# Attention: the first pairs' row maxima, two heads in one tile and one reduction, under another set of planner constants

## The chip, the cores and the metric

The kernel runs on one core of a Trainium2 chip. The metric is device time in microseconds, the median of several executions. Five engines run side by side, each with its own instruction stream in a fixed order: TensorE (PE; its weight loads are PEld), VectorE (DVE), ScalarE (ACT), GpSimd (POOL) and SyncE (SP, which here issues the transfers). They wait for one another by semaphores.

## The reference

Inputs: q, k and v of 4 x 8 heads x 1152 x 64, and the weights of two further layers. Neighbouring rows of q are averaged, so each head has 576 queries and 1152 keys. Per head: scores = q k^T / 8, minus the row maximum, exp, divided by the row sum, times v. The result goes as 2304 tokens x 512 through a dense layer (`h * cos(h)` between two products) and then through 8 experts, of which each token takes the one with the largest gate. Only the attention is touched by the change.

```python
scores = scale * np.matmul(q_pool, k.transpose(0, 1, 3, 2))
scores = scores - np.max(scores, axis=-1, keepdims=True)
attn = np.exp(scores)
attn = attn / (np.sum(attn, axis=-1, keepdims=True) + 1e-09)
return np.matmul(attn, v).astype(np.float32)
```

## The kernel before

**Work.** The 32 heads are taken as 16 pairs; head 0 of a pair lies on partitions 0 to 63, head 1 on 64 to 127. Each pair has two passes over its scores.

The first pass finds the row maxima in rounded copies (`KH`, `QH`, made by ScalarE in `kh` and `qh`). Queries come in four tiles `t` of 128 and a rest of 64 per head (`t` = 4; both heads' rest share one tile through `QT`, made by `qt`), keys in three groups `g` of 384. A tile `(t, g)` is one product per head into a bank of its own of a pair of banks, and VectorE reduces it to the maxima `MX`. `mneg` takes the maximum over the three groups, negated, `pmr` transposes it on TensorE, `mrow` copies it, and `mset` writes it by four small transfers into a row `MR`. For pair 0 tiles 0 to 2 come first and go into `MR` by a quicker way (`pmq`, `mput`); its tiles 3 and 4 follow as a second part (`lo` = 3), whose row is needed for the second half of pair 0's queries alone.

The second pass takes the queries in two halves `hq` of 288 and the keys in nine blocks `j` of 128: `s` puts scores plus the row `MR` into PSUM, `exp` (ScalarE) makes `E`, `es` (GpSimd) adds the nine `E` up for the row sums, `pv` multiplies by v. Per half follow `ob`, `sum`, `ln`, `rcp`, `nr1`, `nr2` and `norm`. GpSimd has the `es` (8 a half), `qadd` (the averaging of q) and `norm`.

**Buffers.** PSUM: two bank pairs for `s`, one bank pair for the maxima (`ps_x`, tag "x"), one bank for `o`, one small. SBUF: 14 `E`, 4 K, 3 Q, 2 each of `KH`, `QH`, `QT`, raw q.

**The first pairs' maxima, as they are now.** In the second part of pair 0 and in all of pair 1 the tile is taken apart: `mx1` (lines 278 to 287) makes the product of one head into one half of a bank pair `T["xe"]` that these steps share, and `red1` (294 to 296) reduces that half, 128 x 384; the halves alternate (`nx % 2`). All other tiles go by `mx` (266 to 276) and `red` (298 to 305), both heads in one bank pair and one reduction of 128 x 768; only tile (4, 2) has one bank.

**Order.** `steps` (37 to 126) lists every step with a due time, an engine, a cost, what it reads and writes and its buffer. The due times count in units of which a pair has six: pair `i` starts at `b = 6*i`, `s` of half `hq` and block `j` is due at `b + 3*hq + j/3`. The rest is set by constants: `p` for the casts, another `p` for the maxima, `SPREAD` over which their 14 tiles are spread, `BEHIND` for `pv`. The conversions of the dense layer's weights (`cabs`, `c1` to `c4`, `chi`, `clo`, stores `cst`) are 32 jobs `n` with due times of their own. `plan` (129 to 184) is a greedy list scheduler: at each turn, per engine, it looks at the steps due at most `AHEAD` after the engine's first pending one, and takes the one with the least of wait x `WAIT` + due time (+ `SWITCH` on TensorE, where the kind of product changes); over all engines the earliest start goes next. It skips steps whose inputs haven't been placed. The order so found is written out as each engine's fixed order; what the planner thinks of durations has no other effect.

```python
late = max(0, t - free[e])*WAIT + P[n][0] + SWITCH*(e == "PE" and P[n][4] != mode)
seen[n] = end[n] + LAND[e] + FETCH.get(p[2], 0)
```

The dense layer and the experts (`moe`) follow the attention in the same program.

Of the kernel before, what the change touches and what calls it, by code (L numbers as in the profile page):

```python
# [8 lines left out]
F32 = mybir.dt.float32  # L9
# [16 lines left out]
COLS, ROWS = "PEc", "PEr"  # L26
LAND = {"PE": 0.27, "ACT": 0.07, "DVE": 0.07, "POOL": 0.07, "SP": 1.9}
FETCH = {"load": 3.0, "loadv": 2.0, "cload": 2.0}
AHEAD = {"PE": 4.5, "DVE": 3.78, "ACT": 3, "POOL": 3.61, "SP": 8.0}
CHANGE = {COLS: 0.2, ROWS: 0.1}  # L30
EARLY = 4
BEHIND = 1.54
SPREAD = 5.1
WAIT, SWITCH = 6.04, 0.85


def steps(NP, NJ, J):


    P, nx = [], 0  # L40

    def at(t, name, args, eng, cost, reads=(), writes=(), buf=None):
        P.append((t, len(P), name, args, eng, cost, list(reads), list(writes), buf))

    tiles = [(t, g) for t in range(4) for g in range(3)] + [(4, 0), (4, 2)]
    for i in range(NP):
        b = 6*i
        first = i == 0
        p = -101 if first else b - 10.75
        early = -200 if i < 2 else b - 20.8  # L50
        at(early, "load", (i, 0), "SP", 0.6, (), [("qr", i, 0)], ("qr", 2, ("qr", i, 0)))
        at(early, "load", (i, 1), "SP", 0.6, (), [("k", i, 0)], ("k", 4, ("k", i, 0)))
        if first:
            at(early, "load", (i, 2), "SP", 0.6, [("k", i, 0)], [("k", i, 1)])
            at(early, "load", (i, 3), "SP", 0.6, [("qr", i, 0)], [("qr", i, 1)])
        at(-200 if first else b - 7, "loadv", (i,), "SP", 0.6, (), [("v", i)], ("v", 3, ("v", i)))
        whole = range(1 + first)
        for x in whole:
            c = ((0.67, 0.33)[x] if first else 1)
            at(p + -0.49 + 9*x, "qadd", (i, x), "DVE" if first and not x else "POOL", 1.45*c, [("qr", i, x)] + [("q", i, 0)]*x, [("q", i, x)], None if x else ("q", 3, ("q", i, 0)))  # L60
            at(p + 0.1 + 9*x, "qh", (i, x), "ACT", 0.2 + 0.47*c, [("q", i, x)] + [("qh", i, 0)]*x, [("qh", i, x)], None if x else ("qh", 2, ("qh", i, 0)))
        for x in range(2):
            c = ((0.48, 0.76)[x] if first else 0.67)
            at(p + (0.1 if first else 0.2 + 0.8*x), "kh", (i, x), "ACT", c, [("k", i, x*first)] + [("kh", i, 0)]*x, [("kh", i, x)], None if x else ("kh", 2, ("kh", i, 0)))
        at(-4 if first else p + 0.98, "qt", (i,), "ACT", 0.48, [("q", i, whole[-1])], [("qt", i % 2)])
        parts = ((0, 3), (3, 5)) if first else ((0, 5),)
        for lo, hi in parts:
            p = (-4 if lo else -100) if first else b - 8.47
            for n, (t, g) in enumerate(tiles):
                if lo <= t < hi:  # L70
                    x = p + n*(0.1 if first else SPREAD/14)
                    ks = [[("kh", i, 0)], [("kh", i, 0), ("kh", i, 1)], [("kh", i, 1)]][g]
                    if t == 4: ks = [("kh", i, 0), ("kh", i, 1), ("qt", i % 2)]
                    else: ks = ks + [("qh", i, x) for x in whole if t == 3 or not x]
                    key = ("x", i, t, g)
                    if lo or i == 1:
                        for h in range(2) if t < 4 else (0, 1)[:3-g]:
                            half = ("x", nx % 2)
                            at(x, "mx1", (i, t, g, h, nx % 2), ROWS, 0.19, ks + [("xe",)]*(nx > 0), [half] + [("xe",)]*(nx == 0), None if nx else ("x", 1, ("xe",)))
                            at(x, "red1", (i, t, g, h, nx % 2), "DVE", 0.56, [half, ("xe",)], [("mx", i, lo)])  # L80
                            nx += 1
                        continue
                    at(x, "mx", (i, t, g), ROWS, 0.35 if (t, g) == (4, 0) else 0.19, ks, [key], ("s", 2, key) if p == -100 and n % 3 else ("x", 1, key))
                    at(x + 0.08, "red", (i, t, g), "DVE", 0.56 if (t, g) == (4, 2) else 0.96, [key], [("mx", i, lo)])
            x = (-2 if lo else p + 2) if first else p + SPREAD
            at(x, "mneg", (i, lo, hi), "DVE", 0.17, [("mx", i, lo)], [("mneg", i, lo)])
            if first and not lo:
                at(x + 0.1, "pmq", (i,), ROWS, 1.2, [("mneg", i, lo)], [("pmr", i, lo)], ("m", 1, ("pmr", i, lo)))
                for h in range(2):
                    at(x + 0.2, "mput", (i, h), ("DVE", "ACT")[h], 0.45, [("pmr", i, lo)], [("mr", i, h - 2)])  # L90
                continue
            at(x + 0.1, "pmr", (i, lo, hi), ROWS, 0.2, [("mneg", i, lo)], [("pmr", i, lo)], ("m", 1, ("pmr", i, lo)))
            at(x + 0.2, "mrow", (i, lo, hi), "DVE", 0.27, [("pmr", i, lo)], [("mrow", i, lo)])
            at(x + 0.2, "mset", (i, lo, hi), "SP", 2.4, [("mrow", i, lo)], [("mr", i, lo)])
        for hq in range(2):
            for j in range(J):
                m = b + 3*hq + j/3
                mr = [("mr", i, x) for x in ([-2, -1] + [3]*hq if first else [0])]
                key = (i, hq, j)
                at(m, "s", key, ROWS, 0.617, [("k", i, x) for x in whole] + [("q", i, x) for x in whole if x < 1 or hq] + mr, [("s", *key)], ("s", 2, ("s", *key)))  # L100
                at(m + 0.17, "exp", key, "ACT", 0.65, [("s", *key)], [("e", *key)], ("e", 14, ("e", *key)))
                if j:
                    at(m + 0, "es", key, *(("DVE", 0.8) if (i, hq) == (NP-1, 1) and j > 4 else ("POOL", 1.45)), [("e", *key)] + [("e", i, hq, 0)]*(j == 1), [("es", i, hq)], ("es", 2, ("es", i, hq)) if j == 1 else None)
                at(m + BEHIND, "pv", key, COLS, 0.486, [("v", i), ("e", *key)], [("o", i, hq)], ("o", 1, ("o", i, hq)) if j == 0 else None)
            m = b + 3*hq + max(3.9, BEHIND + 2.7)
            key = (i, hq)
            at(m + -0.11, "ob", key, "ACT", 0.41, [("o", *key)], [("ob", *key)], ("ob", 2, ("ob", *key)))
            at(m + 0.1, "sum", key, COLS, 0.486, [("es", *key)], [("sum", *key)], ("m", 1, ("sum", *key)))
            at(m + 0.5, "ln", key, "ACT", 0.5, [("sum", *key)], [("ln", *key)], ("ln", 2, ("ln", *key)))
            at(m + 0.46, "rcp", key, "ACT", 0.44, [("ln", *key)], [("r0", *key)], ("r0", 2, ("r0", *key)))  # L110
            at(m + 0.3, "nr1", key, "DVE", 0.46, [("sum", *key), ("r0", *key)], [("nr", *key)], ("nr", 2, ("nr", *key)))
            at(m + 0.6, "nr2", key, "DVE", 0.46, [("r0", *key)], [("nr", *key)])
            at(m + 0.54, "norm", key, "POOL", 0.95, [("nr", *key), ("ob", *key)], [("xT", *key)])
    for n in range(NJ):
        x = 10.76 + 3.01*n if n < 27 else 89 + 1.2*(n - 27)
        at(x - 5, "cload", (n,), "SP", 0.6, (), [("ct", n)], ("ct", 2, ("ct", n)))
        at(x, "cabs", (n,), "ACT", 0.65, [("ct", n)], [("ca", n)], ("m", 1, ("ca", n)))
        for c in range(1, 5):
            at(x + 0, f"c{c}", (n,), "DVE", 0.69, [("ct", n)], [("ca", n)])
        at(x + 0.27, "chi", (n,), "ACT", 0.58, [("ca", n)], [("co", n)], ("co", 2, ("co", n)))  # L120
        at(x + 0, "clo", (n,), "DVE", 0.69, [("ca", n)], [("co", n)])
        at(x + 0.1, "cst", (n,), "SP", 1.2, [("co", n)], [("ws", n)])
        f = n - 4*(n//8) - 4
# [63 lines left out]
def attention(nc, tc, q, k, v, xT, ident, w_in, w_out, ws, x2d, W1):  # L187
# [7 lines left out]
    KG = 384  # L195
# [3 lines left out]
    with ExitStack() as ctx:  # L199
# [75 lines left out]
                for x, gg in enumerate(range(g, min(g+2, 3))):  # L275
                    nc.tensor.matmul(p[:, x, :KG], lhsT=QT[i % 2], rhs=KH[:, gg*KG:(gg+1)*KG], start=True, stop=True)

        def mx1(i, t, g, h, b):

            if "xe" not in T:  # L280
                T["xe"] = ps_x.tile([128, 2, 512], F32, tag="x", name="pmx")
            p = T["xe"][:, b, :KG]
            KH, QH = T["kh", i], T["qh", i]
            if t < NT4:
                nc.tensor.matmul(p, lhsT=QH[R[h], t*128:(t+1)*128], rhs=KH[R[h], g*KG:(g+1)*KG], start=True, stop=True)
            else:
                nc.tensor.matmul(p, lhsT=QT[i % 2], rhs=KH[:, (g+h)*KG:(g+h+1)*KG], start=True, stop=True)

        def maxima(i):
            if ("mx", i) not in T:  # L290
                T["mx", i] = sm.tile([128, 27], F32, tag="MX", name="MX")
            return T["mx", i]

        def red1(i, t, g, h, b):
            o = 24+g+h if t == NT4 else 3*(2*t+h)+g
            nc.vector.reduce_max(maxima(i)[:, o:o+1], T["xe"][:, b, :KG], axis=AX.X)

        def red(i, t, g):
            p = T.pop(("x", i, t, g))
            out = maxima(i)  # L300
            if t < NT4:
                nc.vector.reduce_max(out.rearrange("p (w g) -> p w g", g=3)[:, 2*t:2*t+2, g], p[:, :, :KG], axis=AX.X)  # L302
            else:
# [721 lines left out]
```

## Time and profile before

| | us |
|---|---|
| median of 3 runs | 1232.14 |
| lowest, highest | 1231.37, 1232.37 |
| profiled execution, its own time | 1230.01 |
| its span, first to last instruction | 1228.3 |
| attention within it | to about 482 |

The span is the part of the profiled execution that the trace covers; 1.7 us lie around it. Rows of the timeline give the start (us from the start of the span), the duration, engine, line, operation, output <- input, the number of instructions merged into the row, and in brackets the engine's idle time before it and who ended it. A row of several instructions lasts from the first start to the last end. Rows of groups give the busy time and the mean of one in ns. TensorE's products overlap, and their ends are modelled.

### The profile page before, as it was taken

Reading aid. Unit: us, or ns where it says so; the run is one execution under the profiler, and the core shown is the slowest. Engines: PE = TensorE matmul, PEld = TensorE weight load, DVE = VectorE, ACT = ScalarE, POOL = GpSimd, SP = SyncE. Lnnn points to the kernel's source line nnn. Section 1 sums busy time; section 2 is a strip of 40 time slices with the busy share of each in tenths; the row PEclk is TensorE's granted clock in tenths of the full one; section 3 lists DMA queues with packets and bytes.
Section 4 is the critical chain, followed back from the end, with each engine's and each line's share of the span. In section 5 each row is a group of like instructions: output and inputs, shape, how many; then the busy total and the mean of one; then the engine's idle time right before and its main releaser. Section 6 shows DMA issues by size and latency. Waiting matters only on the chain. (4 is left out here: it accounts for less than half of the span.)

```text
span 1228.3 us, 22291 instructions
## 1 busy us (share of the span) xinstructions
PE 1189.6 (97%) x8158; PEld 932.2 (76%) x8158; DVE 891.7 (73%) x1916; ACT 764.0 (62%) x1528; POOL 469.1 (38%) x414
## 2 busy tenths in 40 slices
PE   4799999999999999999999999999999999999997
PEld 2466666666666556989898889889987888888886
DVE  4568887887788767777767767767777877777761
ACT  2266666666666667666566565565575877677751
POOL 2489999999999886000000000000003121112100
PEclk9999999999999999999999999999999999999999
DMA  6034466434433236600000000000047997889710
GB/s 256 18 94 127 157 220 209 152 128 146 143 127 108 89 115 245 259 19 1 18 19 1 19 1 18 19 1 18 26 160 252 398 319 265 273 274 308 265 56 6
DMA packets 70942, 163.73 MB, mean 133 GB/s; under 512 B 7669, under 2 KB 24813, under 8 KB 68784
## 3 DMA queue, kind: packets, MB, share of 16 engines
q1 hardware_dynamic: 66832, 150.92, 35.5%
q0 software_dynamic: 4000, 11.38, 2.6%
q8 instruction: 64, 1.05, 0.3%
q14 instruction: 46, 0.38, 0.1%
HBM read 135.65 MB, written 28.39 MB: 134 GB/s over the span
## 5 line engine op out<-in xcount | busy, mean ns | idle before, releaser
L362 POOL TENSOR_TENSOR es<-es,E 128x576 f32<-128x576 f32 x220 | 313.7, 1426 | 27.4 <-ACT E L355 14.9
L355 ACT ACTIVATE E<-s 128x576 f32<-128x576 f32 x288 | 183.2, 651 | 109.6 <-PE s L351 102.2
L897 PE MATMUL h<-xh,wf 128*128 128x256 f32 x1152 | 231.9, 285 | 0.1
L918 PE MATMUL po<-wf,g 128*128 128x512 f32 x864 | 222.3, 394 | 1.3 <-ACT g L909 0.6
L302 DVE TENSOR_REDUCE MX<-pmx 128x2 f32<-128x768 f32 x177 | 168.7, 956 | 55.8 <-PE pmx L273 55.7
L754 POOL DMA_INDIRECT xg<-x2d,idx x25 | 26.9, 1075 | 465.5 <-ACT ar L902 388.8
L349 PE MATMUL s<-Q,K 64*128 64x288 f32 x1152 | 193.8, 419 | 1.5 <-ACT E L355 1.5
L897 PEld LDWEIGHTS h<-xh,wf 128*128 128x128 f32 x1152 | 188.1, 191 | 6.6 <-issue 1.8
L918 PEld LDWEIGHTS po<-wf,g 128*128 128x128 f32 x864 | 153.4, 189 | 28.1 <-ACT g L909 1.3
L743 DVE TENSOR_TENSOR w<-raw,w 128x1024 fp32r<-128x1024 f32 x128 | 154.6, 1220 | 22.2 <-ACT w L742 20.2
L897 PE MATMUL h<-xl,wf 128*128 128x256 f32 x576 | 163.2, 283 | 0.0
L368 PE MATMUL o<-E,vt 128*64 128x288 f32 x1152 | 161.2, 414 | 0.0
L351 PE MATMUL s<-MR,ON 64*128 64x288 f32 x576 | 148.5, 508 | 0.0
L742 ACT CAST w<-raw 128x1024 fp32r<-128x1024 f32 x128 | 132.9, 1052 | 20.5 <-DMA raw<-in_moe_w_dram 11.9
L821 PE MATMUL po<-w,hh 128*128 128x512 f32 x600 | 144.4, 393 | 1.0 <-DVE hh L792 0.6
L821 PEld LDWEIGHTS po<-w,hh 128*128 128x128 f32 x600 | 110.5, 188 | 24.1 <-DVE hh L792 1.5
L906 ACT ACTIVATE ar<-ar 128x256 f32<-128x256 f32 x144 | 60.1, 417 | 96.7 <-DVE ar L905 96.3
L368 PEld LDWEIGHTS o<-E,vt 128*64 128x64 f32 x1152 | 75.2, 136 | 58.2 <-issue 15.3
L349 PEld LDWEIGHTS s<-Q,K 64*128 64x128 f32 x1152 | 96.6, 187 | 25.8 <-ACT E L355 11.5
L897 PEld LDWEIGHTS h<-xl,wf 128*128 128x128 f32 x576 | 110.0, 191 | 3.7
L788 PE MATMUL ph<-xh,w 128*128 128x256 f32 x576 | 109.7, 287 | 1.0 <-ACT xh L715 1.0
L825 POOL DMA_INDIRECT out_dram<-ob,idx x25 | 27.2, 1090 | 201.9 <-ACT ob L824 183.8
(204 smaller groups left out, 1849.2 us busy)
## 6 DMA issues: line engine op xcount, KB each, us to landing
raw<-in_moe_w_dram SPq DMA_DIRECT2D x128, 512.0 KB
wf<-ws SPq DMA_DIRECT2D x16, 1024.0 KB
vt<-in_v_dram SPq DMA_DIRECT2D x16, 576.0 KB
qr<-in_q_dram SPq DMA_DIRECT2D x15, 576.0 KB
K<-in_k_dram SPq DMA_DIRECT2D x15, 576.0 KB
cv_t<-in_moe_w_in_dram SPq DMA_DIRECT2D x16, 512.0 KB
ws<-cv_o SPq DMA_DIRECT2D x32, 256.0 KB
cv_t<-in_moe_w_out_dram SPq DMA_DIRECT2D x16, 512.0 KB
```

The source lines that it names most:

```text
L302: nc.vector.reduce_max(out.rearrange("p (w g) -> p w g", g=3)[:, 2*t:2*t+2, g], p[:, :, :KG], axis=AX.X)
L349: nc.tensor.matmul(p[:, h, :NQ], lhsT=T["k", i][R[h], j*128:(j+1)*128], rhs=T["q", i][R[h], qs], start=True, stop=False)
L351: nc.tensor.matmul(p[:, h, :NQ], lhsT=ON[R[h]], rhs=MR[i % 3][R[h], qs], start=False, stop=True)
L355: nc.scalar.activation(e, T.pop(("s", i, hq, j))[:, :, :NQ], AF.Exp, scale=1.0/16)
L362: (nc.vector if (i, hq) == (NP-1, 1) and j > 4 else nc.gpsimd).tensor_add(T["es", i, hq], T["e", i, hq, 0] if j == 1 else T["es", i, hq], ...
L368: nc.tensor.matmul(T["o", i, hq][64*h:64*h+64], lhsT=T["v", i][:, h, j], rhs=T["e", i, hq, j][:, h], start=(j == 0), stop=(j == J-1))
L742: nc.scalar.copy(w[:, 0], t)
L743: nc.vector.tensor_sub(w[:, 1], t, w[:, 0])
L788: nc.tensor.matmul(ph, lhsT=wt[k][:, a, m*128:(m+1)*128], rhs=x[k//2][y][:, k % 2], start=(c == 0), stop=(c == 3*KC-1))
L821: nc.tensor.matmul(po, lhsT=hs[m][:, y, q*128:(q+1)*128], rhs=wt[4 + m//2][:, a, (m % 2)*512:(m % 2)*512+512], start=(c == 0), stop=(c == ...
L897: nc.tensor.matmul(h, lhsT=w[:, a, k*128:(k+1)*128], rhs=x[k//2][y][:, k % 2], start=(n == 0), stop=(n == 3*KC-1))
L918: nc.tensor.matmul(pos[c][t], lhsT=g[:, y, t*128:(t+1)*128], rhs=W1[f][:, b, 512:], start=(f == 0 and i == 0), stop=(f == FT-1 and i == 2))
```

## The change

`mx1`, `red1` and the shared `T["xe"]` go away. The second part of pair 0 and all of pair 1 now take `mx` and `red` like the others: two products into one bank pair, one reduction, one such bank pair in all. With that, most constants of the planner change. The core of the diff (the remaining lines are further due times of the same kind):

```diff
-AHEAD = {"PE": 4.5, "DVE": 3.78, "ACT": 3, "POOL": 3.61, "SP": 8.0}
+AHEAD = {"PE": 4.54, "DVE": 4.7, "ACT": 3, "POOL": 3.07, "SP": 8.0}
-BEHIND = 1.54
+BEHIND = 1.39
-WAIT, SWITCH = 6.04, 0.85
+WAIT, SWITCH = 6.19, 0.7
...
-        p = -101 if first else b - 10.75
+        p = -101 if first else b - 12.5
...
-            at(p + -0.49 + 9*x, "qadd", ...
+            at(p + -0.71 + 9*x, "qadd", ...
...
-        at(-4 if first else p + 0.98, "qt", ...
+        at(-4 if first else p + 1.96, "qt", ...
...
-            p = (-4 if lo else -100) if first else b - 8.47
+            p = (-4 if lo else -100) if first else b - 8.37
...
-                    if lo or i == 1:
-                        for h in range(2) if t < 4 else (0, 1)[:3-g]:
-                            half = ("x", nx % 2)
-                            at(x, "mx1", (i, t, g, h, nx % 2), ROWS, 0.19, ...
-                            at(x, "red1", (i, t, g, h, nx % 2), "DVE", 0.56, [half, ("xe",)], [("mx", i, lo)])
-                            nx += 1
-                        continue
                     at(x, "mx", (i, t, g), ROWS, 0.35 if (t, g) == (4, 0) else 0.19, ks, [key], ("s", 2, key) if p == -100 and n % 3 else ("x", 1, key))
-                    at(x + 0.08, "red", (i, t, g), "DVE", 0.56 if (t, g) == (4, 2) else 0.96, [key], [("mx", i, lo)])
+                    at(x + -0.65, "red", (i, t, g), "DVE", 0.56 if (t, g) == (4, 2) else 0.96, [key], [("mx", i, lo)])
...
-                at(m + 0.17, "exp", ...
+                at(m + 0.43, "exp", ...
-                    at(m + 0, "es", ...
+                    at(m + -0.1, "es", ...
...
-            m = b + 3*hq + max(3.9, BEHIND + 2.7)
+            m = b + 3*hq + max(3.62, BEHIND + 2.7)
...
-        x = 10.76 + 3.01*n if n < 27 else 89 + 1.2*(n - 27)
+        x = 10.21 + 3.04*n if n < 27 else 89 + 1.2*(n - 27)
...
-            at(x + 0, f"c{c}", ...
+            at(x + 0.18, f"c{c}", ...
-        at(x + 0.27, "chi", ...
+        at(x + 0, "chi", ...
```

## Rows read from the trace of the kernel before

**Rows 1.** Busy time by stretch: length, then busy us (x instructions) per engine, clock

```profile
19.12:34.40 15.28, 8.60 (x18) 4.00 (x18) 6.60 (x12) 5.69 (x13) 0.00 (x0) 1.00 0.24 90
34.40:57.82 23.42, 19.20 (x111) 11.27 (x113) 12.99 (x26) 6.51 (x10) 12.69 (x9) 1.00 0.08 24
73.20:404.00 330.80, 330.26 (x2618) 205.04 (x2616) 264.21 (x362) 222.51 (x397) 312.83 (x255) 1.00 0.46 150
```

**Rows 2.** Waits of GpSimd, 37 to 73.2 us, then 73.2 to 404

```profile
POOL es L362 <- ACT E L355: 28.9, 7, 18.3
...
POOL es L362 <- ACT E L355: 8.2, 22, 0.9
```

**Rows 3.** Timeline of GpSimd, the first additions

```profile
37.05 1.43 POOL L362 TENSOR_TENSOR es<-E 128x576 f32<-128x576 f32 x1 [18.34 <-ACT E L355]
39.01 7.41 POOL L362 TENSOR_TENSOR es<-es,E 128x576 f32<-128x576 f32 x5 [0.54 <-ACT E L355]
...
71.84 1.41 POOL L248 TENSOR_TENSOR Q<-qr 128x576 f32<-128x576 f32 x1
73.20 1.46 POOL L362 TENSOR_TENSOR es<-E 128x576 f32<-128x576 f32 x1
```

**Rows 4.** Timeline of VectorE, `mneg` of two pairs in a row

```profile
193.09 0.18 DVE L314 TENSOR_REDUCE mneg<-MX 128x9 f32<-128x27 f32 x1
...
220.41 0.18 DVE L314 TENSOR_REDUCE mneg<-MX 128x9 f32<-128x27 f32 x1
```

**Rows 5.** Timeline of TensorE, 19 to 35 us

```profile
19.12 0.69 PE L285 MATMUL pmx<-KH,QH 64*128 64x384 f32 x2 [1.59 <-ACT QH L260]
...
19.61 1.16 PE L349 MATMUL s<-Q,K 64*128 64x288 f32 x4
...
20.93 0.68 PE L285 MATMUL pmx<-KH,QH 64*128 64x384 f32 x1
...
22.26 0.68 PE L285 MATMUL pmx<-KH,QH 64*128 64x384 f32 x1 [0.65 <-DVE MX L296]
...
34.41 1.33 PE L349 MATMUL s<-Q,K 64*128 64x288 f32 x3
```

**Rows 6.** Groups of VectorE instructions in the attention: busy us, mean ns

```profile
L302 DVE TENSOR_REDUCE MX<-pmx 128x2 f32<-128x768 f32 x177 | 168.7, 956 | 55.8 <-PE pmx L273 55.7
...
L296 DVE TENSOR_REDUCE MX<-pmx 128x1 f32<-128x384 f32 x36 | 19.4, 555 | 20.0 <-PE pmx L285 15.2 <-PE pmx L287 4.8
```

**Rows 7.** Timeline of several engines, 39 to 62 us

```profile
39.00 0.44 PE L285 MATMUL pmx<-KH,QH 64*128 64x384 f32 x2
...
39.48 1.02 DVE L296 TENSOR_REDUCE MX<-pmx 128x1 f32<-128x384 f32 x2 [0.54 <-PE pmx L285]
...
40.56 0.44 PE L285 MATMUL pmx<-KH,QH 64*128 64x384 f32 x1 [0.51 <-DVE MX L296]
...
57.82 0.18 DVE L314 TENSOR_REDUCE mneg<-MX 128x9 f32<-128x27 f32 x1
...
61.19 0.51 SPq L333 DMA_DIRECT2D MR<-mrow  x1
```

**Rows 8.** Timeline of TensorE, two double tiles in a later pair

```profile
396.43 0.43 PE L273 MATMUL pmx<-KH,QH 64*128 64x384 f32 x2
...
398.39 0.44 PE L273 MATMUL pmx<-KH,QH 64*128 64x384 f32 x2
```

**Rows 9.** Timeline, the first load of K and the cast that reads it

```profile
1.60 1.05 SPq L236 DMA_DIRECT2D K<-in_k_dram  x2
...
4.76 0.51 ACT L254 CAST KH<-K 128x384 fp32r<-128x384 f32 x1 [2.66 <-DMA K<-in_k_dram]
```

**Rows 10.** Timeline of TensorE, last `s` of pair 0 and first of pair 1

```profile
67.00 0.76 PE L349 MATMUL s<-Q,K 64*128 64x288 f32 x4
...
67.72 0.71 PE L349 MATMUL s<-Q,K 64*128 64x288 f32 x4
```

**Rows 11.** Costliest groups of the page: the exponentials

```profile
L355 ACT ACTIVATE E<-s 128x576 f32<-128x576 f32 x288 | 183.2, 651 | 109.6 <-PE s L351 102.2
```

More of the change, by code (lines that the diff above doesn't have):

```diff
@@ L28 @@
 FETCH = {"load": 3.0, "loadv": 2.0, "cload": 2.0}
-AHEAD = {"PE": 4.5, "DVE": 3.78, "ACT": 3, "POOL": 3.61, "SP": 8.0}
+AHEAD = {"PE": 4.54, "DVE": 4.7, "ACT": 3, "POOL": 3.07, "SP": 8.0}
 CHANGE = {COLS: 0.2, ROWS: 0.1}
 EARLY = 4
-BEHIND = 1.54
+BEHIND = 1.39
 SPREAD = 5.1
-WAIT, SWITCH = 6.04, 0.85
+WAIT, SWITCH = 6.19, 0.7
 def steps(NP, NJ, J):
-    P, nx = [], 0
+    P = []
     def at(t, name, args, eng, cost, reads=(), writes=(), buf=None):
@@ L59, in steps @@
             c = ((0.67, 0.33)[x] if first else 1)
-            at(p + -0.49 + 9*x, "qadd", (i, x), "DVE" if first and not x else "POOL", 1.45*c, [("qr", i, x)] + [("q", i, 0)]*x, [("q", i, x)], None if x else ("q", 3, ("q", i, 0)))
+            at(p + -0.71 + 9*x, "qadd", (i, x), "DVE" if first and not x else "POOL", 1.45*c, [("qr", i, x)] + [("q", i, 0)]*x, [("q", i, x)], None if x else ("q", 3, ("q", i, 0)))
             at(p + 0.1 + 9*x, "qh", (i, x), "ACT", 0.2 + 0.47*c, [("q", i, x)] + [("qh", i, 0)]*x, [("qh", i, x)], None if x else ("qh", 2, ("qh", i, 0)))
@@ L64, in steps @@
             at(p + (0.1 if first else 0.2 + 0.8*x), "kh", (i, x), "ACT", c, [("k", i, x*first)] + [("kh", i, 0)]*x, [("kh", i, x)], None if x else ("kh", 2, ("kh", i, 0)))
-        at(-4 if first else p + 0.98, "qt", (i,), "ACT", 0.48, [("q", i, whole[-1])], [("qt", i % 2)])
+        at(-4 if first else p + 1.96, "qt", (i,), "ACT", 0.48, [("q", i, whole[-1])], [("qt", i % 2)])
         parts = ((0, 3), (3, 5)) if first else ((0, 5),)
         for lo, hi in parts:
-            p = (-4 if lo else -100) if first else b - 8.47
+            p = (-4 if lo else -100) if first else b - 8.37
             for n, (t, g) in enumerate(tiles):
@@ L75, in steps @@
                     key = ("x", i, t, g)
-                    if lo or i == 1:
-                        for h in range(2) if t < 4 else (0, 1)[:3-g]:
-                            half = ("x", nx % 2)
-                            at(x, "mx1", (i, t, g, h, nx % 2), ROWS, 0.19, ks + [("xe",)]*(nx > 0), [half] + [("xe",)]*(nx == 0), None if nx else ("x", 1, ("xe",)))
-                            at(x, "red1", (i, t, g, h, nx % 2), "DVE", 0.56, [half, ("xe",)], [("mx", i, lo)])
-                            nx += 1
-                        continue
                     at(x, "mx", (i, t, g), ROWS, 0.35 if (t, g) == (4, 0) else 0.19, ks, [key], ("s", 2, key) if p == -100 and n % 3 else ("x", 1, key))
-                    at(x + 0.08, "red", (i, t, g), "DVE", 0.56 if (t, g) == (4, 2) else 0.96, [key], [("mx", i, lo)])
+                    at(x + -0.65, "red", (i, t, g), "DVE", 0.56 if (t, g) == (4, 2) else 0.96, [key], [("mx", i, lo)])
             x = (-2 if lo else p + 2) if first else p + SPREAD
@@ L100, in steps @@
                 at(m, "s", key, ROWS, 0.617, [("k", i, x) for x in whole] + [("q", i, x) for x in whole if x < 1 or hq] + mr, [("s", *key)], ("s", 2, ("s", *key)))
-                at(m + 0.17, "exp", key, "ACT", 0.65, [("s", *key)], [("e", *key)], ("e", 14, ("e", *key)))
+                at(m + 0.43, "exp", key, "ACT", 0.65, [("s", *key)], [("e", *key)], ("e", 14, ("e", *key)))
                 if j:
-                    at(m + 0, "es", key, *(("DVE", 0.8) if (i, hq) == (NP-1, 1) and j > 4 else ("POOL", 1.45)), [("e", *key)] + [("e", i, hq, 0)]*(j == 1), [("es", i, hq)], ("es", 2, ("es", i, hq)) if j == 1 else None)
+                    at(m + -0.1, "es", key, *(("DVE", 0.8) if (i, hq) == (NP-1, 1) and j > 4 else ("POOL", 1.45)), [("e", *key)] + [("e", i, hq, 0)]*(j == 1), [("es", i, hq)], ("es", 2, ("es", i, hq)) if j == 1 else None)
@@ L104, in steps @@
                 at(m + BEHIND, "pv", key, COLS, 0.486, [("v", i), ("e", *key)], [("o", i, hq)], ("o", 1, ("o", i, hq)) if j == 0 else None)
-            m = b + 3*hq + max(3.9, BEHIND + 2.7)
+            m = b + 3*hq + max(3.62, BEHIND + 2.7)
             key = (i, hq)
-            at(m + -0.11, "ob", key, "ACT", 0.41, [("o", *key)], [("ob", *key)], ("ob", 2, ("ob", *key)))
-            at(m + 0.1, "sum", key, COLS, 0.486, [("es", *key)], [("sum", *key)], ("m", 1, ("sum", *key)))
-            at(m + 0.5, "ln", key, "ACT", 0.5, [("sum", *key)], [("ln", *key)], ("ln", 2, ("ln", *key)))
@@ L110, in steps @@
[L110 to L113, printed above, removed]
+            at(m + 0, "ob", key, "ACT", 0.41, [("o", *key)], [("ob", *key)], ("ob", 2, ("ob", *key)))
@@ new lines, in steps @@
+            at(m + 0.15, "sum", key, COLS, 0.486, [("es", *key)], [("sum", *key)], ("m", 1, ("sum", *key)))
+            at(m + 0.75, "ln", key, "ACT", 0.5, [("sum", *key)], [("ln", *key)], ("ln", 2, ("ln", *key)))
+            at(m + 0.74, "rcp", key, "ACT", 0.44, [("ln", *key)], [("r0", *key)], ("r0", 2, ("r0", *key)))
+            at(m + 0.21, "nr1", key, "DVE", 0.46, [("sum", *key), ("r0", *key)], [("nr", *key)], ("nr", 2, ("nr", *key)))
+            at(m + 0.64, "nr2", key, "DVE", 0.46, [("r0", *key)], [("nr", *key)])
@@ L114, in steps @@
+            at(m + 0.42, "norm", key, "POOL", 0.95, [("nr", *key), ("ob", *key)], [("xT", *key)])
     for n in range(NJ):
-        x = 10.76 + 3.01*n if n < 27 else 89 + 1.2*(n - 27)
+        x = 10.21 + 3.04*n if n < 27 else 89 + 1.2*(n - 27)
         at(x - 5, "cload", (n,), "SP", 0.6, (), [("ct", n)], ("ct", 2, ("ct", n)))
@@ L118, in steps @@
         for c in range(1, 5):
-            at(x + 0, f"c{c}", (n,), "DVE", 0.69, [("ct", n)], [("ca", n)])
-        at(x + 0.27, "chi", (n,), "ACT", 0.58, [("ca", n)], [("co", n)], ("co", 2, ("co", n)))
+            at(x + 0.18, f"c{c}", (n,), "DVE", 0.69, [("ct", n)], [("ca", n)])
+        at(x + 0, "chi", (n,), "ACT", 0.58, [("ca", n)], [("co", n)], ("co", 2, ("co", n)))
         at(x + 0, "clo", (n,), "DVE", 0.69, [("ca", n)], [("co", n)])
@@ L276, in mx, with red @@
                     nc.tensor.matmul(p[:, x, :KG], lhsT=QT[i % 2], rhs=KH[:, gg*KG:(gg+1)*KG], start=True, stop=True)
[L278 to L289, printed above, removed]
+        def red(i, t, g):
+            p = T.pop(("x", i, t, g))
             if ("mx", i) not in T:
                 T["mx", i] = sm.tile([128, 27], F32, tag="MX", name="MX")
[L292 to L300, printed above, removed]
+            out = T["mx", i]
             if t < NT4:
```

## The prediction

> **What bounds the kernel now.** The edit sits in the attention part, so I first cut the trace there with the busy-time-by-stretch view [rows 1]. Between 73.20 and 404 us TensorE is busy 330.26 of 330.80 us and GpSimd 312.83. A matmul's end is modelled, so the first figure alone proves little; the waits of GpSimd [rows 2] add that it waited for work only 8.2 us in those 331. The rest of its gap is the step from one instruction to the next: five additions take 7.41 us in a row [rows 3], 1.48 each. VectorE (264.21) and ScalarE (222.51) have room. A pair of heads takes 27.32 us there, from one `mneg` to the next [rows 4], and in it both TensorE and GpSimd are near full: nothing can take much off this stretch, at most the 8.2 us.
>
> The start is another matter. From 19.12 to 34.40 us TensorE is busy 8.60 of 15.28 us and GpSimd does nothing [rows 1]; up to 73.20 GpSimd waits 28.9 us for exponentials, 18.3 of it ahead of its first addition at 37.05 [rows 2, 3]. The timeline tells why [rows 5]. The first score step `s` of pair 0 runs at 19.61, the next one at 34.41; in between TensorE does one single-head product of the maxima after another, at 20.93, 22.26 and so on, one in 1.33 us, and each is released by the reduction before it. The two halves of the bank pair are meant to alternate, so that a product runs beside the other half's reduction, but the product at 22.26 is released by the reduction just ended (VectorE is named as the releaser): where product and reduction are issued in turn, product (0.68) and reduction (0.555, [rows 6]) add up. Only where two products are issued together does the pair go in one cycle, 1.56 us from 39.00 to 40.56 [rows 7]. The planner, though, costs a half at 0.19 and 0.56 us and lets halves overlap, so it found the maxima ready almost at once and put eleven more of them ahead of the second `s`. Pair 1's maxima end at 57.82 [rows 7].
>
> **The change, part by part.** (1) Removed: 36 single reductions of 0.555 us [rows 6] and the 36 single products' turns. Added: 19 double ones (5 for the rest of pair 0, 14 for pair 1), 17 of 0.956 and 2 of about 0.555. That is 20.0 us of VectorE against 17.4, and the products stay 36. The busy time hardly matters; the turns do.
>
> (2) The cycle of a double tile is not in this start, but in the later pairs. Lower bound: VectorE waits 0.54 us for two products and then reduces [rows 7]; 0.54 + 0.956 = 1.50. Upper bound: in the steady part, where a batch of `pv` lies between, 396.43 to 398.39 is 1.96 [rows 8]. I take 1.70, nearer the start's own two-product cycle of 1.56, but with a score step or a `pv` in the way now and then. A single-bank tile saves 0.40 of it: 1.30. The first three run while a product still takes 0.685 us instead of 0.44 [rows 5, 7], 0.25 more each (the granted clock reads 1.00, the 2.4 GHz level, in both stretches [rows 1], so I go by the durations). Sum: 19.12 + 17 x 1.70 + 2 x 1.30 + 0.8 = 51.4 us for the end of pair 1's maxima, against 57.82.
>
> (3) The order. With one buffer, the next tile's product can't be ready for some 1.3 us by the planner's own costs (0.27 to land, 0.96, 0.07). A wait costs 6.19 per us in its choice, so 8 units, while the maxima's due times are only about 3 units ahead of `s`: it must put an `s` or a `pv` into each gap. Then the second `s` follows the first within some 3 us instead of 15, and the first addition, which in the trace comes 2.6 us after its `s` began (34.41 to 37.05), starts at about 24.5 (second `s` at 22, plus 2.6) instead of 37.05. GpSimd's 16 additions of pair 0 (23.7 us), one `qadd` (1.41) and the first norm (taken as no longer) end near 51.
>
> (4) What is late next is pair 1's row of maxima. In the trace it takes 3.9 us from `mneg` (57.82) to the end of the last of four transfers' issue (61.19 + 0.51) [rows 7]; the landing isn't shown, and lies between nothing and the 3.2 us from the first K issue to the cast that reads it (1.60 to 4.76, [rows 9]); I take 2.5, nearer that row, as a transfer's landing too. So pair 1's first `s` can run at 51.4 + 6.4 = 57.8, against 67.72 [rows 10]: 9.9 us sooner. GpSimd starts pair 1 two steps (1.3) and an exponential (0.65, [rows 11], and hops) later, at 60.4 against 73.20 [rows 3]: 12.8 us. Pair 0's second half needs a row too: five tiles end at 28.0 (19.12 + 4 x 1.70 + 1.30 + 0.8), its row lands 6.4 later at 34.4, when the eight additions of the first half still run to 36.3 (24.5 + 8 x 1.48); a wait of a microsecond or two there is hidden by GpSimd's slack up to 60.4. From pair 1 on both engines are full, and what is gained stays gained; between the two figures I take 11.
>
> (5) The new constants move the due times of nearly every step; no count of instructions changes. One unit is 27.32/6 = 4.55 us. Per pair `qadd` goes 1.97 units ahead on GpSimd, `qh`, two `kh` 1.75 ahead and the two copies of `qt` 0.77 ahead on ScalarE, past exponentials; loads of q and k keep their time, v too. Reductions may come 0.73 earlier, `exp` 0.26 later, `pv` 0.15 earlier; conversions start 2.5 us sooner and come at 3.04 instead of 3.01 units, their two 256 or one 512 KB stores on SP with them. VectorE and ScalarE have 66 and 108 us free in the steady part, which hide this. I cost it at nothing. Bounds: a gain of 8.2 us (all of GpSimd's waits gone), and a loss of an exponential's length, 0.65, ahead of one first addition per pair, if a step on ScalarE is put before it: 0.65 x 13 = 8.5.
>
> **Sum.** 1230.01 - 11 = 1219.0 for the profiled execution. That one lies 2.1 us under the median of the runs shown (1232.14) and 1.4 under the fastest, so against the median I say 1221. The part after attention is issued unchanged and moves as a block.
>
> **A rule against it.** The product at 22.26 finds TensorE idle for 0.65 us and is released by the reduction of the other bank, so the halves aren't overlapped there [rows 5]. The Trainium skill's page "PSUM — Partial Sum Buffer", summary of rules, says that a PSUM bank read while matmuls run calls for a different bank and for guarding by bank. The old form follows it, the new one reads both banks at once and stops the products for it; by that rule the time would rise as in rival (d). The trace does not bear it out: the guard is by the whole tile, and what the rule would save isn't there to be given up.
>
> **Rivals.** (a) Only the cycle improves, not the order: the maxima still go ahead of `s`, or the halves of pair 0 wait for their rows with GpSimd idle. For it: the due times of maxima remain ahead. Against: the gap of 1.3 us. At the 1.96 cycle the maxima end at 55.8 (17 x 1.96 + 2.6 + 0.8 + 19.1), 2.0 sooner; with part of the order 4: 1228. (b) The gain is eaten: what GpSimd gains at the start it waits for later, 11/13 = 0.85 us in each of 13 pairs, 1232; the start has no such wait now, but GpSimd's 8.2 us show that the chain exponential to addition is tight. (c) Slower: `qadd` stands too early. It is due at b - 13.2, but its Q buffer (three of them) is last read by `s` of three pairs before, due at b - 12.3; today it runs at 71.84, after that `s` at 67.00. In GpSimd's fixed order everything behind it, additions and norms, would stand still, while the exponentials fill their 14 buffers. Price: an addition's time, 1.43 [rows 3], times 13 is 18.6, less 11: 1240; it decides from 0.85 us per pair. Against: the planner passes over a step that isn't ready, and the additions themselves trail `s` by some 2 us, so the buffer is mostly free in time. (d) The halves do overlap once the products come early enough, as the pairs issued together suggest (two reductions in 1.02 us at 39.48, [rows 7]). Then the old form's floor is VectorE's own pace, 36 x 0.555 = 20 us, its end 39.1, and a double tile's 51.4 would be 12 us later: 1244. This is the case of the rule above. The end measured in the trace, 57.82, leaves it 0.01.
>
> **How the numbers follow.** The forecast has 0.62; its own range is 1212 (cycle 1.50, GpSimd 16 sooner, half of the 8.2) to 1229 (cycle 1.96 with the new order, some loss later). (a) 0.14, (b) 0.09, (c) 0.14, (d) 0.01. About 0.2% (2.5 us) is what a measurement here can tell from no change. Faster: 0.62 + 0.14 = 0.76; same: (b), 0.09; slower: (c) and (d), 0.15. The range of 8 in 10 goes from 1211 to 1233, holding the forecast, (a) and most of (b), and leaving (c), (d) and the forecast's edges outside.
>
> **What would show it.** In the changed profile: the second `s` before 25 us and GpSimd's first addition at 23 to 27; double reductions every 1.5 to 2.0 us from 19 on; pair 1's `mneg` at 48 to 56; pair 1's first addition near 60; the 27.3 us period unchanged. I am wrong if GpSimd's waits after 73 us exceed some 16 us, if a `qadd` shows idle time ahead of it released by TensorE, if the period passes 28.1, or if the second `s` still comes after 30.

## The result and the profile after

| | before | after |
|---|---|---|
| median, us | 1232.25 (4 runs) | 1214.18 (4 runs) |
| profiled execution, us | 1230.01 | 1213.6 |
| its span | 1228.3 | 1211.9 |

The ratio is 0.986, 95% interval 0.9843 to 0.9877: 18 us or 1.4% faster, where 11 were forecast; 1214.2 lies inside the stated range of 1211 to 1233. In the traces the difference is 16.4 us, since the profiled execution of before lies 2.2 us under its median and that of after 0.6.

Busy time by stretch, after, in the stretches of [rows 1] (length, then busy us and instructions of PE, PEld, DVE, ACT, POOL):

```profile
19.12:34.40 15.28, 14.18 (x80) 8.77 (x82) 8.21 (x11) 9.44 (x20) 7.68 (x6) 1.00 0.25 91
...
73.20:404.00 330.80, 330.63 (x2615) 204.78 (x2613) 266.11 (x366) 224.72 (x402) 310.30 (x254) 1.00 0.46 149
```

TensorE's first 15 us went from 8.60 busy to 14.18 and GpSimd's from nothing to 7.68. The timelines of TensorE, VectorE and GpSimd, after, answer to [rows 3, 5, 7, 10]:

```profile
20.67 1.16 PE L324 MATMUL s<-Q,K 64*128 64x288 f32 x4
...
55.27 0.65 PE L324 MATMUL s<-Q,K 64*128 64x288 f32 x4
```

```profile
39.80 0.96 DVE L277 TENSOR_REDUCE MX<-pmx 128x2 f32<-128x768 f32 x1 [0.54 <-PE pmx L266]
...
49.86 0.18 DVE L289 TENSOR_REDUCE mneg<-MX 128x9 f32<-128x27 f32 x1
...
205.88 0.18 DVE L289 TENSOR_REDUCE mneg<-MX 128x9 f32<-128x27 f32 x1
233.15 0.18 DVE L289 TENSOR_REDUCE mneg<-MX 128x9 f32<-128x27 f32 x1
```

```profile
25.56 1.43 POOL L337 TENSOR_TENSOR es<-E 128x576 f32<-128x576 f32 x1 [6.78 <-ACT E L330]
...
57.43 1.45 POOL L337 TENSOR_TENSOR es<-E 128x576 f32<-128x576 f32 x1 [3.53 <-ACT E L330]
```

The second score step comes at 20.67 instead of 34.41, the first addition at 25.56 instead of 37.05. From 29 to 46 us a double tile takes 1.50 us, 0.54 of waiting and 0.96 of reduction, from tile to tile. Pair 1's `mneg` is at 49.86 instead of 57.82, its first `s` at 55.27 instead of 67.72, its first addition at 57.43 instead of 73.20. The period, from one pair's `mneg` to the next, is 27.27 us, where it was 27.32 [rows 4].

GpSimd's waits from 60 to 391 us, after:

```profile
POOL xT L375 <- DVE nr L367: 7.2, 18, 0.5
POOL es L337 <- ACT E L330: 2.5, 5, 0.9
POOL Q L241 <- PE s L324: 0.3, 1, 0.3
```

Their sum, 10.0 us, is much as it was (8.2 in [rows 2]); they only changed place, from the first additions of a half to the norms. The experiments say why the sum stays.

### The profile page after: what moved, and what is told of

The parts are those of the page before. It is cut to its first block, busy times and chain, and to the rows that moved or that the text cites. A ratio compares the mean times of both kernels' runs of the same rounds, so it can differ in the third digit from the quotient of the medians.

```text
span 1211.9 us, 22290 instructions
## 1 busy us (share of the span) xinstructions
PE 1182.6 (98%) x8158; PEld 928.1 (77%) x8158; DVE 890.4 (73%) x1899; ACT 763.1 (63%) x1528; POOL 468.4 (39%) x414
## 3 DMA queue, kind: packets, MB, share of 16 engines
q8 instruction: 64, 1.05, 0.4%
## 5 line engine op out<-in xcount | busy, mean ns | idle before, releaser
L337 POOL TENSOR_TENSOR es<-es,E 128x576 f32<-128x576 f32 x220 | 312.0, 1418 | 17.2 <-ACT E L330 3.3
L277 DVE TENSOR_REDUCE MX<-pmx 128x2 f32<-128x768 f32 x192 | 183.2, 957 | 67.0 <-PE pmx L266 66.1
L343 PEld LDWEIGHTS o<-E,vt 128*64 128x64 f32 x1152 | 75.3, 136 | 57.4 <-issue 15.9
L800 POOL DMA_INDIRECT out_dram<-ob,idx x25 | 27.8, 1113 | 201.2 <-ACT ob L799 170.4
```

The lines of the kernel that those rows point to most:

```text
L337: (nc.vector if (i, hq) == (NP-1, 1) and j > 4 else nc.gpsimd).tensor_add(T["es", i, hq], T["e", i, hq, 0] if j == 1 else T["es", i, hq], ...
L343: nc.tensor.matmul(T["o", i, hq][64*h:64*h+64], lhsT=T["v", i][:, h, j], rhs=T["e", i, hq, j][:, h], start=(j == 0), stop=(j == J-1))
```

## The experiments

Theory A: the planner took the halves as overlapping, which as coded they did not; its order starved the scores, and the double tile mends order and turns at once. Rival B: the new constants did it. Rival C: only VectorE's fewer turns count. Each run was timed beside the kernel before on the same chip. The last columns give, in us of the trace, the second `s`, pair 1's `mneg`, pair 1's first addition, and the time T from that addition to the dense layer's first product. T leaves out the start, which differs between executions of one order by itself: up to pair 1's first addition e10_q15_late has the order of the kernel after, and reaches it 1.15 us sooner.

| run | median | against before | ratio, 95% | 2nd `s` | `mneg` | addition | T |
|---|---|---|---|---|---|---|---|
| before | 1231 to 1232 | | | 34.41 | 57.82 | 73.20 | 406.4 |
| after | 1214.18 | -18.1 | 0.9843 to 0.9877 | 20.67 | 49.86 | 57.43 | 404.2 |
| e1_const | 1234.73 | +3.7 | 1.002 to 1.0049 | 34.84 | 59.09 | 74.86 | 408.5 |
| e2_form | 1218.27 | -12.7 | 0.9885 to 0.9918 | 20.51 | 49.71 | 57.28 | 407.5 |
| e3_truth | 1224.23 | -6.8 | 0.9931 to 0.9964 | 20.16 | 59.28 | 67.33 | 406.0 |
| e4_split | 1218.57 | -12.4 | 0.9888 to 0.9921 | 27.26 | 46.55 | 61.94 | 406.7 |
| e5_split_new | 1219.85 | -11.3 | 0.989 to 0.9923 | 27.11 | 45.80 | 61.58 | 406.8 |
| e6_es_dve | 1237.71 | +6.5 | 1.0033 to 1.0067 | 21.17 | 50.33 | 57.90 | 428.4 |
| e7_casts_old | 1224.27 | -6.9 | 0.9926 to 0.9959 | 20.95 | 50.84 | 59.02 | 413.3 |
| e8_jobs_old | 1215.13 | -16.1 | 0.9844 to 0.9877 | 20.70 | 49.85 | 57.42 | 404.7 |
| e9_q15_early | 1215.31 | -15.9 | 0.9856 to 0.9886 | 20.89 | 51.13 | 58.80 | 406.1 |
| e10_q15_late | 1216.55 | -14.7 | 0.9875 to 0.9907 | 20.65 | 48.72 | 56.28 | 408.3 |
| e11_pool_extra | 1214.08 | -17.2 | 0.9846 to 0.9883 | 20.75 | 49.97 | 57.54 | 404.8 |
| e12_pe_extra | 1230.53 | -0.7 | 0.9983 to 1.0003 | 20.93 | 50.52 | 58.56 | 418.4 |

**Form and constants apart.** e1_const is the kernel after with the branch of `mx1` and `red1` put back; e2_form is the kernel before without it:

```diff
-                    if lo or i == 1:
...
-                        continue
```

> The new constants alone; the first pairs' maxima stay single halves. Theory A (the planner costs halves as overlapping, which they don't, so it starves the scores at the start; the double tile mends that, and the constants matter by a few us): the second score step still after 30 us, 1226 to 1238. Rival B (the constants brought the gain): 1213 to 1219.

> The double tile alone, under the old constants. A: second score step before 25 us, GpSimd's first addition at 24 to 28, pair 1's mneg at 48 to 52, 1214 to 1221. B: 1227 or more. Rival C (only VectorE's fewer turns count, the order does not): mneg 6 to 8 us sooner, the second score step still late, 1224 to 1227.

The form alone brings 12.7 of the 18 us and the whole of the start; the constants alone lose 3.7. B falls. A's marks came, but for GpSimd's first addition, at 22.83 a little sooner than 24 to 28. With the form the constants are worth another 4 to 5 us, 3.3 of it in T (407.5 to 404.2); without it they make T longer (408.5 against 406.4), most of it in one pair, which takes 31.00 us from `mneg` to `mneg` (141.17 to 172.17).

**Order and turns apart.** e3_truth leaves the single halves, but tells the planner that they are one buffer:

```diff
-                            half = ("x", nx % 2)
+                            half = ("x", 0)
```

> The kernel before, its single halves and old constants, but the planner is told that both halves are one buffer. Order alone: second score step before 25 us and first addition before 28. A expects the 36 single turns, now with score steps in the gaps, at 1.1 to 1.5 us each, pair 1's mneg at 59 to 72 and its first addition at 69 to 82: 1228 to 1241, so order alone is not enough. If the order alone made the gain: 1214 to 1220.

Order alone moved the second `s` to 20.16 and brought 6.8 us, which A had put at 3 at most: a miss, and short of the 11 or more of order as the whole cause. `mneg` came at 59.28, as bad as before, yet pair 1's additions began 5.9 us sooner, since pair 0 was done earlier (its last addition ends at 55.88 instead of 71.88). So of the start's 16 us some 6 are order, and the other 10 come with the earlier row of pair 1. C falls too.

e4_split keeps the old order and makes the halves overlap: the single-bank tiles come from a pool that takes the place of the two-bank one for these steps.

```diff
-                T["xe"] = ps_x.tile([128, 2, 512], F32, tag="x", name="pmx")
-            p = T["xe"][:, b, :KG]
+                T["xe", b] = ps_of("half").tile([128, 512], F32, tag=f"x{b}", name="pmx")
+            p = T["xe", b][:, :KG]
```

> The kernel before with old constants, but the two halves are two tiles of one bank each, so that nothing ties a product to the other half's reduction. A: products and reductions overlap, one half in 0.6 to 0.75 us, the second score step at 26 to 30, pair 1's mneg at 41 to 47, 1214 to 1222: the old plan was right for halves that overlap. If the halves can't overlap for another reason (a bank or an engine): cycle still 1.1 to 1.33, mneg near 58, 1230 to 1234.

VectorE's timeline of e4_split:

```profile
32.86 5.44 DVE L306 TENSOR_REDUCE MX<-pmx 128x1 f32<-128x384 f32 x10 [0.69 <-PE pmx L295]
```

Ten reductions in 5.44 us, one in 0.544, without a wait: with a tile to each bank the halves do overlap, and the wait of [rows 5] was between the steps of one tile, as coded, and nothing of the chip. `mneg`, at 46.55, is 3.2 us sooner than with the double tile under the same constants (49.71), but the second `s` comes 7 us later, and the time is that of e2_form. The Trainium skill's rule of guarding by bank ("PSUM — Partial Sum Buffer", summary of rules) agrees with e4_split; it is worth no more here than the double tile with the better order. Overlapping halves in a better order were not run. e5_split_new does the same under the new constants (e1_const with the edit of e4_split):

> The new constants, with single halves that truly overlap (two tiles of one bank). If the start's gain comes from the maxima's turns and the order, this start is about that of the split halves under the old constants (pair 1's first addition at 59 to 63) and the tail that of the new constants: 1212 to 1219. If the new constants need the double tile: 1222 or more.

Its start is that of e4_split. The time is 0.9 us above the expectation, a miss: the new constants' shorter T did not come with this form (406.8), in which one pair takes 29.11 us (127.91 to 157.02).

**Which engine sets the period.** e6_es_dve moves the last addition of each half from pair 1 on to VectorE:

```diff
-(nc.vector if (i, hq) == (NP-1, 1) and j > 4 else nc.gpsimd).tensor_add(
+(nc.vector if (i, hq) == (NP-1, 1) and j > 4 or i and j == J-1 else nc.gpsimd).tensor_add(
```

> The kernel after, with the last addition of each half (from pair 1 on) moved from GpSimd to VectorE. Per pair GpSimd loses 2 x 1.48 = 3.0 us and VectorE gains 1.5 to 3. If GpSimd alone sets the 27.3 us period, it falls to 25 to 26.3 and the time to 1184 to 1204. If TensorE's own work sets it too, the period stays above 26.8 and the time at 1207 to 1216. If VectorE becomes late (its maxima are next): slower than 1217.

It was slower, and doesn't decide: the planner's 0.8 us for the moved addition is not what it took, and VectorE became late. From 73.2 to 390 us TensorE's products wait 8.1 us for VectorE, in the kernel after not at all by the same view, and the period is about 29 us. The group of these additions on VectorE, 120 to 390 us, two of them, and an addition on GpSimd:

```profile
L337 DVE TENSOR_TENSOR es<-es,E 128x576 f32<-128x576 f32 x19 | 23.8, 1255 | 0.9 <-POOL es L337 0.3
```

```profile
215.91 1.99 DVE L337 TENSOR_TENSOR es<-es,E 128x576 f32<-128x576 f32 x1
...
229.28 0.75 DVE L337 TENSOR_TENSOR es<-es,E 128x576 f32<-128x576 f32 x1
```

```profile
215.83 1.45 POOL L337 TENSOR_TENSOR es<-E 128x576 f32<-128x576 f32 x1
```

The addition takes 1255 ns in the mean, 748 at the least and 1987 at the most. The one at 215.91 begins while GpSimd's runs, to 217.28, and ends 0.62 us after it; the one at 229.28 falls where GpSimd stands idle (229.20 to 230.37). In the kernel before, from 465 to 490 us, when GpSimd is nearly done, four such additions take 751 ns in the mean. The Trainium skill's page "SBUF — State Buffer", section on the two separate sides, says that of a VectorE instruction with two SBUF inputs and a GpSimd one that reads SBUF, whichever starts first blocks the other for the whole instruction. These rows agree for VectorE; for GpSimd, its next four additions, from 217.36, take 6.28 us, where four in a row take 5.90 in the kernel after (at 202.53).

e11_pool_extra adds a fill on GpSimd ahead of each norm, e12_pe_extra a repeated product on TensorE in each half; both leave the planner and the results alone.

```diff
+            nc.gpsimd.memset(extra, 0.0)
...
+                if h == 0:
+                    nc.tensor.matmul(p[:64], lhsT=ones, rhs=T["es", i, hq][:, h], start=True, stop=True)
```

> The kernel after, with a fill of 128x256 of its own on GpSimd ahead of each half's norm, some 0.3 us, 0.6 a pair, unknown to the planner. If GpSimd sets the 27.3 us period: 0.5 to 0.6 longer a pair, 7 to 9 us in all (1221 to 1224). If TensorE sets it, GpSimd's 0.8 us of waits a pair take it up: under 3 us (1214 to 1217).

> The kernel after, with the row-sum product of head 0 issued twice in each half, some 0.25 us of TensorE, 0.5 a pair, unknown to the planner; the same sums are written. If TensorE sets the period: 6 to 8 us more (1220 to 1223). If GpSimd alone sets it: under 2 us.

GpSimd's groups from 60 to 390 us in e11_pool_extra, then VectorE's `mneg` in e11_pool_extra and in e12_pe_extra:

```profile
L373 POOL MEMSET extra<- 128x256 f32 x24 | 7.4, 309 | 0.0
```

```profile
206.22 0.18 DVE L290 TENSOR_REDUCE mneg<-MX 128x9 f32<-128x27 f32 x1
233.53 0.18 DVE L290 TENSOR_REDUCE mneg<-MX 128x9 f32<-128x27 f32 x1
```

```profile
212.42 0.18 DVE L289 TENSOR_REDUCE mneg<-MX 128x9 f32<-128x27 f32 x1
240.64 0.18 DVE L289 TENSOR_REDUCE mneg<-MX 128x9 f32<-128x27 f32 x1
```

0.62 us more a pair on GpSimd leave the period at 27.31 and the time where it was; GpSimd's waits from 60 to 390 us fall from 10.0 us to 2.1, about by the 7.4 of the fills. The repeated product makes the period 28.22, 0.95 more, or 0.48 for each half, twice what I had guessed; T grows by 14.2, and the time by 16.4 instead of 6 to 8. TensorE's products wait only 1.0 us there from 73.2 to 390, so that it is TensorE's work that grew, and not a wait behind the longer row sums. TensorE sets the period, and GpSimd's busy time (312.83 of 330.80 us before) hid that: its waits, some 0.8 us a pair, are what TensorE's pace leaves over.

**The end of the attention.** T is 2.2 us shorter after than before. In the kernel before, ScalarE stands 2.49 us ahead of the dense layer's first cast `xh`, and the exponentials behind it. The trace names the last `qadd` as what that cast waits for; what ties the two is not shown. Timeline of ScalarE, before and after:

```profile
404.62 1.14 ACT L715 CAST xh<-xT 128x512 fp32r<-128x512 f32 x2 [2.49 <-POOL Q L248]
```

```profile
382.64 1.14 ACT L690 CAST xh<-xT 128x512 fp32r<-128x512 f32 x2 [1.06 <-POOL Q L241]
```

Theory A2 is that the earlier `qadd` shortens T, against the conversions' new due times. e7_casts_old puts all casts' due times back, e8_jobs_old the conversions':

```diff
-        p = -101 if first else b - 12.5
+        p = -101 if first else b - 10.75
-            at(p + -0.71 + 9*x, "qadd", ...
+            at(p + -0.49 + 9*x, "qadd", ...
-        at(-4 if first else p + 1.96, "qt", ...
+        at(-4 if first else p + 0.98, "qt", ...
```

```diff
-        x = 10.21 + 3.04*n if n < 27 else 89 + 1.2*(n - 27)
+        x = 10.76 + 3.01*n if n < 27 else 89 + 1.2*(n - 27)
-            at(x + 0.18, f"c{c}", ...
+            at(x + 0, f"c{c}", ...
-        at(x + 0, "chi", ...
+        at(x + 0.27, "chi", ...
```

> The kernel after, with the due times of qadd, of the casts and of qt as before. Theory A2 (the last 4 us of the gain come from the last qadd standing earlier, so that ScalarE is no longer held 2.5 us ahead of the dense layer's first cast): ScalarE waits over 2 us for qadd near 390 to 405, pair 13 to 15 lose the 4 us again, 1216 to 1220. Rival (the conversions' due times did it): within 1 us of the kernel after.

> The kernel after, with the conversions' due times as before. Theory A2: within 1.5 us of the kernel after, no wait over 2 us of ScalarE for qadd. Rival (the conversions' due times made the tail shorter): 1216 to 1220, GpSimd's waits after 390 us back at 4 to 6 us.

The conversions' due times are worth nothing that can be measured. The casts' are worth more than A2 said: the period of e7_casts_old is 27.59 us (209.99 to 237.58), 0.3 longer, beside the wait for `qadd`, which is 4.1 us there. So two things are mixed in it; why the period grew was not tried. e9_q15_early and e10_q15_late move the last pair's `qadd` alone, in e2_form and in the kernel after:

```diff
-            at(p + -0.49 + 9*x, "qadd", ...
+            at(p + -0.49 + 9*x - (2 if i == NP-1 else 0), "qadd", ...
...
-            at(p + -0.71 + 9*x, "qadd", ...
+            at(p + -0.71 + 9*x + (1.97 if i == NP-1 else 0), "qadd", ...
```

> The double tile under the old constants, with the qadd of the last pair alone due 2 units sooner. Theory A2 (the dense layer's first cast on ScalarE stands behind that qadd, and holds the exponentials): ScalarE's wait for qadd falls from 2.4 to under 1.2 us, GpSimd's waits in the tail fall by 1.5 or more, and the time by 1.5 to 4 us against the double tile alone (1214.5 to 1217). Rival (the other constants made the tail): no change, within 1 us of 1218.3.

> The kernel after, with the qadd of the last pair alone due 1.97 units later. A2: ScalarE waits 2 us or more for it again, and 1.5 to 4 us are lost (1215.5 to 1218). Rival: within 1 us of the kernel after.

ScalarE in e2_form, e9_q15_early and e10_q15_late:

```profile
390.81 0.62 ACT L708 CAST xh<-xT 128x512 fp32r<-128x512 f32 x1 [2.36 <-POOL Q L241]
```

```profile
384.32 1.14 ACT L708 CAST xh<-xT 128x512 fp32r<-128x512 f32 x2
```

```profile
388.93 1.14 ACT L690 CAST xh<-xT 128x512 fp32r<-128x512 f32 x2 [3.05 <-POOL Q L241]
```

Sooner, the wait is gone and T is 1.4 us shorter (3.0 by the medians); later, the wait is 3.05 and T 4.1 longer (2.4 by the medians, 3.4 against before). The sign and the wait are as A2 says; by the medians the size is only bounded, and the intervals of the pairs just touch. In the trace e9_q15_early's dense layer starts no sooner (464.92 against 464.76), as its start was 1.5 us later by itself.

The size can be read where the cast stands, between the `mneg` of pair 13 and that of pair 14. In the kernel after:

```profile
369.74 0.18 DVE L289 TENSOR_REDUCE mneg<-MX 128x9 f32<-128x27 f32 x1
...
397.37 0.18 DVE L289 TENSOR_REDUCE mneg<-MX 128x9 f32<-128x27 f32 x1
```

| run | the cast's wait for `qadd`, us | from `mneg` to `mneg`, us |
|---|---|---|
| before | 2.49 | 29.97 (384.41 to 414.38) |
| e4_split | 2.49 | 29.98 |
| e2_form | 2.36 | 29.19 |
| e3_truth | 1.99 | 29.12 |
| e10_q15_late | 3.05 | 31.77 |
| e7_casts_old | 4.13 | 30.77 |
| after | 1.06 | 27.63 |
| e1_const | 1.05 | 27.64 |
| e5_split_new | 1.06 | 27.70 |
| e8_jobs_old | 1.05 | 27.64 |
| e9_q15_early | none | 27.75 |

With a wait of about 2 us or more this stretch takes 29.1 to 31.8 us, with 1.1 or less 27.6 to 27.8, whatever the form of the maxima. Against before that is 2.3 us, all that T lost. Of the 3.3 us of T between e2_form and the kernel after it is 1.6; the other 1.7 were not traced to a constant. The constants alone shorten this stretch too, and lose more than that in earlier pairs. No run beat the kernel after by more than its interval.

## Why the prediction was right, and where it was off

- **The size.** 11 us were forecast; 18.0 came up to the dense layer's first product: 15.8 at the start, by pair 1's first addition, where 9.9 to 12.8 were worked out, and 2.2 behind it, where nothing was. That the range's own low end, 1212, lay so near is in part luck: its cycle of 1.50 and its 16 us came, its half of GpSimd's waits did not.
- **What was misplaced at the start** (order, step 3): as put. The second `s` "at 22" was at 20.67, GpSimd's first addition "at 24.5" at 25.56. e3_truth shows that the planner's belief alone made the order; e4_split that the belief would have been true with another tile.
- **The cycle** (step 2) was mis-sized: 1.70 taken, 1.50 measured, the lower bound itself, since two score steps or two `pv` fit in a gap without holding the next product. The first tiles were slower than the 0.25 added (reductions at 19.71, 22.43, 24.18 and 26.31). `mneg` "at 51.4" came at 49.86.
- **The row of pair 1** (step 4): 6.4 us taken from `mneg` to the first `s`, 5.4 measured (49.86 to 55.27); the issue ended at 53.45, so the landing took at most 1.8, not 2.5. So 12.4 us for TensorE instead of 9.9, and 15.8 instead of 12.8 for GpSimd. Counted by `mneg`, 14.7 us were left at 369.74 against 384.41.
- **"From pair 1 on both engines are full"** was half right: the conclusion held, but e11 and e12 show that TensorE sets the period and GpSimd has some 0.8 us a pair left. GpSimd's 8.2 us of waits were not there to be given back, since TensorE's pace keeps them.
- **The constants** (step 5), "I cost it at nothing": this term failed. With the double tile they brought 4 to 5 us (e2_form to after), 1.6 of it through the earlier `qadd`; for the rest the cause is open. The wait that it shortens stood in the trace of before, at 404.62, and I hadn't looked for the program's next stage in ScalarE's stream.
- **"The part after attention moves as a block"**: nearly. The dense layer's first product came 18.0 us sooner (479.64 to 461.62), the end 16.4; of the 1.6 us lost on the way I have not shown the cause, and they may be none of the change: from that product to the end the fourteen traces take between 748.2 and 752.7 us, before 748.7 and after 750.3.
- **Rivals.** (a) fell with the start, (b) with the 14.7 us that were left at 369.74. (c) was wrong in its sign: in the kernel after GpSimd waits 0.3 us in all for TensorE ahead of a `qadd`, and the earlier `qadd` is a gain. By the letter one of the prediction's signs of being wrong showed in these 0.3 us; they are too few to matter. (d): the overlap is real when each half has its own tile (e4_split), and even then, in the old order, no faster than the double tile.

## What to carry to other kernels

A list scheduler's order is only as good as its picture of what waits for what: where the code shares one tile, the plan must say one buffer, and a trace in which each product is released by the reduction just ended shows the mismatch. When two engines look full, a small dummy on each tells which of them sets the pace, sooner than any busy share does. Before a due time is costed at nothing, look in every engine's stream for the first instruction of the program's next stage and what it waits for.

## What the runs showed that I had not expected

GpSimd, 94% busy, took 0.62 us a pair more without loss (1214.08 against 1214.18). A repeated f32 product of 288 columns for one head cost 0.48 us of TensorE each, about as much as a whole `pv` step with both heads (16 of its instructions, four steps, take 2.11 us at 212.18 in the kernel after). An addition on VectorE took up to 1.99 us instead of 0.75 when it met one of GpSimd's.
